# Retention and two feed-forward layers on one core: one written order, retention in pairs, smaller first-layer groups

## The chip, the core and the metric

The kernel runs on one core of a Trainium2 chip. A core has a matrix engine (TensorE, PE in the rows, with PEld for its weight loads), VectorE (DVE), ScalarE (ACT), GpSimd (POOL) and SyncE (SP), which issues the transfers (DMA). Matmuls write PSUM, eight banks of 2 KB per partition; all else works in SBUF. The metric is device time in microseconds (us); the span runs from the first to the last instruction of one profiled execution.

## The reference

```
for t in range(768):                                   # retention, 2 batches, 8 heads of 64
    state = gamma * state + k[t] (outer) v[t]
    y[t] = q[t] @ state / sqrt(64)
x = y as 1536 tokens x 512
h = x @ w_in   (512 x 2048);  g = softplus(h);  x = g @ w_out   (2048 x 512)
h = x @ w_in2  (512 x 2048);  g = h * sigmoid(h);  out = g @ w_out2
```

q, k, v are single precision, the weights double precision.

## The kernel before

**Retention.** The 768 positions are cut into 6 pieces of 128; with 2 batches that makes 12 chunks (chunk n is piece n // 2 of batch n % 2). For each chunk TensorE makes the scores of all heads (`att_scores`, L156: 8 matmuls, each over one half of the rows, which write two PSUM tiles), VectorE multiplies them by a decaying mask (L160), and TensorE multiplies them with v (the within-chunk part, `att_out`, L170: 8 matmuls, each into one half of the output partitions). To this it adds the across-chunk part, the scaled q times the state of all earlier pieces (L180: 4 full matmuls), in the same PSUM tile `py`. GpSimd scales q (L104) and k (L114). `att_state` multiplies scaled k with v in a PSUM tile (L130), and VectorE adds that to a block-diagonal state `sbd` in SBUF (L140, L142). ScalarE and VectorE split the result into a rounded part and the rest (xhi L195, xlo L196).

**Feed-forward.** Every operand is a pair (hi, lo), and a product is three matmuls. A step is one slice of 128 of the 2048 hidden channels for one block of 512 tokens (4 chunks): a first product of twelve matmuls into a PSUM tile `h` (`gemm1`, L277), an activation on ScalarE that writes it twice (`act1`, L293 and L294), the difference on VectorE (`act2`, L300), and, LAG = 2 steps later, a second product of twelve matmuls into four PSUM banks `acc` (`gemm2`, L319). Slices come in groups of 4; within a group the three blocks follow one another, and at the end of a block `acc` is added into `part` (`evacuate`, L334 to L338). There are 2 layers x 16 slices x 3 blocks = 96 steps.

**Weights.** Each of 64 weight tiles (32 slices, in and out) is loaded as raw 64-bit words (512 KB, three buffers) and converted: one ScalarE operation (L221), six on VectorE (`w_upper`, `w_lower`), one rounding copy on ScalarE (`w_split`, L256). `_convert_plan` says at which step.

**Order.** The opening and the first NFREE = 10 steps are ordered by a scheduler, which may mix independent parts on an engine; from step 10 on each engine follows the written order. All transfers go through SyncE's queue. The chunks' retention lies in the first steps: step i also carries chunk i + 5.

## Time and profile before

| | us |
|---|---|
| median of 3 runs | 602.47 (602.04 to 604.19) |
| the profiled execution | 602.17 |
| its span | 600.4 |
| TensorE busy | 585.1 (97%), 2946 matmul records |
| VectorE busy | 362.6 (60%) |
| ScalarE busy | 196.8 (33%) |
| GpSimd busy | 43.9 (7%) |
| transfers | 51.61 MB, 86 GB/s over the span |

A single-precision matmul shows as two records. A matmul's record is longer than the distance to the next, since matmuls are pipelined, so lengths of TensorE's work are read from starts. The granted clock says what share of full speed TensorE was given: 1.00 is 2.4 GHz, 0.50 is 1.2 GHz.

### The profile page before, as it was taken

The page shows a single profiled execution, that of the slowest core. Times are in us where ns is not written, and L with a number is a line of the kernel's source. Part 1 is how long each engine was busy: PE and PEld are TensorE (multiplying, and loading weights), DVE is VectorE, ACT ScalarE, POOL GpSimd, SP SyncE. Part 2 cuts the span into 40 slices and gives each one's busy share as a digit, 9 for nine tenths or more (in the row PEclk, how much of TensorE's full clock was granted, in tenths as well). Part 3 has the DMA queues.
Part 4 walks back from the last instruction along what each step waited for, and adds up shares of the span by engine and source line. Part 5 has one row for each costly group of instructions (what it writes and reads, how often), then busy time and mean ns, then how long its engine had stood idle before and what let it go on. Part 6 is the DMA issues. An engine that isn't in the chain of part 4 may idle for free.

```text
span 600.4 us, 7352 instructions
## 1 busy us (share of the span) xinstructions
PE 585.1 (97%) x2946; PEld 477.8 (80%) x2946; DVE 362.6 (60%) x622; ACT 196.8 (33%) x358; POOL 43.9 (7%) x36
## 2 busy tenths in 40 slices
PE   6999989999999999999999999999999999999997
PEld 3777767888888888888888888888888888888885
DVE  3899974145764757556766886365655775473332
ACT  1333322134322332333344543343333233332220
POOL 1343110000000000000032230000000000000000
PEclk9899989999999999999999999999999999999999
DMA  8883540012310311122221112131112122100111
GB/s 331 346 306 122 208 153 27 1 35 71 98 44 34 106 64 53 59 71 70 71 70 36 70 72 70 36 105 50 58 69 72 68 72 70 36 0 1 70 71 70
DMA packets 14145, 51.61 MB, mean 86 GB/s; under 512 B 1696, under 2 KB 1696, under 8 KB 12960
## 3 DMA queue, kind: packets, MB, share of 16 engines
q1 hardware_dynamic: 14112, 51.15, 23.8%
q8 instruction: 23, 0.38, 0.3%
q14 instruction: 10, 0.08, 0.0%
HBM read 48.00 MB, written 3.15 MB: 85 GB/s over the span
## 4 chain that ended last, share of the span: by engine, by line
PE 90%; DVE 6%; DMA 1%; issue 1%; ACT 0%; SPq 0%; DVEq 0%
PE acc L319 43%; PE h L277 42%; PE py L170 3%; PE py L180 2%; DMA mask<-in_mask 1%; DVE scm L160 1%; PE kv L130 1%; PE sc L156 1%; DVE sbd L142 1%; DVE m L238 1%; DVE glo L300 1%; DVE m L239 1%; DVE xlo L196 1%; DVE a L229 1%; DVE wlo L246 0%
## 5 line engine op out<-in xcount | busy, mean ns | idle before, releaser
L293 ACT ACTIVATE ghi<-h 128x512 fp32r<-128x512 f32 x96 | 57.4, 598 | 324.7 <-PE h L277 324.7
L226 DVE TENSOR_SCALAR z<-z 128x512 uint32<-128x512 uint32 x64 | 28.4, 444 | 115.7 <-ACT z L221 115.7
L300 DVE TENSOR_TENSOR glo<-t,ghi 128x512 fp32r<-128x512 f32 x96 | 66.6, 694 | 47.6 <-ACT t L294 47.6
L277 PE MATMUL h<-xhi,wlo 128*128 128x512 f32 (+1 forms) x196 | 76.0, 388 | 0.5 <-ACT xhi L195 0.5
L277 PE MATMUL h<-xlo,whi 128*128 128x512 f32 (+1 forms) x196 | 75.8, 387 | 0.0
L319 PE MATMUL acc<-ghi,wlo 128*128 128x512 f32 x192 | 75.8, 395 | 0.0
L277 PE MATMUL h<-xhi,whi 128*128 128x512 f32 (+1 forms) x196 | 75.7, 386 | 0.0
L319 PE MATMUL acc<-ghi,whi 128*128 128x512 f32 x192 | 74.9, 390 | 0.0
L319 PE MATMUL acc<-glo,whi 128*128 128x512 f32 x192 | 74.8, 390 | 0.0
L277 PE MATMUL h<-yhi,wlo 128*128 128x512 f32 x192 | 74.7, 389 | 0.0
L277 PE MATMUL h<-ylo,whi 128*128 128x512 f32 x192 | 74.7, 389 | 0.0
L277 PE MATMUL h<-yhi,whi 128*128 128x512 f32 x192 | 74.7, 389 | 0.0
L319 PE MATMUL acc<-whi,glo 128*128 128x512 f32 x192 | 74.7, 389 | 0.0
L319 PE MATMUL acc<-wlo,ghi 128*128 128x512 f32 x192 | 74.7, 389 | 0.0
L319 PE MATMUL acc<-whi,ghi 128*128 128x512 f32 x192 | 74.7, 389 | 0.0
L334 DVE TENSOR_TENSOR part<-acc,part 128x512 f32<-128x512 f32 x72 | 49.0, 691 | 34.3 <-PE acc L319 33.9
L294 ACT ACTIVATE t<-h 128x512 f32<-128x512 f32 x96 | 56.9, 593 | 0.0
L221 ACT ACTIVATE z<-raw 128x512 f32<-128x512 f32 x64 | 42.3, 663 | 24.1 <-DVE wlo L246 14.1
L256 ACT ACTIVATE whi<-a 128x512 fp32r<-128x512 f32 x64 | 40.4, 632 | 22.9 <-DVE a L229 22.9
L246 DVE SCALAR_TENSOR_TENSOR wlo<-m,z 128x512 fp32r<-128x512 int32 x64 | 44.8, 700 | 2.1
L239 DVE SCALAR_TENSOR_TENSOR m<-raw,m 128x512 uint32<-128x512 uint32 x64 | 44.3, 692 | 1.8
L229 DVE SCALAR_TENSOR_TENSOR a<-raw,z 128x512 uint32<-128x512 uint32 x64 | 44.3, 692 | 1.8
(42 smaller groups left out, 718.9 us busy)
## 6 DMA issues: line engine op xcount, KB each, us to landing
raw<-in_wts SPq DMA_DIRECT2D x64, 512.0 KB, 3.3
att<-in_att SPq DMA_DIRECT2D x9, 1024.0 KB, 6.5
out<-part SPq DMA_DIRECT2D x12, 256.0 KB, 2.1
att<-in_att SPq DMA_DIRECT2D x2, 768.0 KB, 10.6
qs<-in_qs SPq DMA_DIRECT2D x5, 256.0 KB, 6.2
att<-in_att SPq DMA_DIRECT2D x2, 512.0 KB, 6.0
mask<-in_mask SPq DMA_DIRECT2D x1, 512.0 KB, 8.6
att<-in_att SPq DMA_DIRECT2D x2, 256.0 KB, 9.3
```

What stands on the lines that cost most here:

```text
L221: nc.scalar.activation(out=z, in_=raw_t[u][:, :, 1].bitcast(F32), func=AF.Copy, scale=2.0**-112)
L226: nc.vector.tensor_scalar(out=z, in0=z, scalar1=3, scalar2=4, op0=ALU.logical_shift_left, op1=ALU.bitwise_or)
L229: nc.vector.scalar_tensor_tensor(out=a, in0=raw[:, :, 1], scalar=0x80000000, in1=z, op0=ALU.bitwise_and, op1=ALU.bitwise_or)
L239: nc.vector.scalar_tensor_tensor(out=m, in0=raw[:, :, 1], scalar=23, in1=m, op0=ALU.logical_shift_left, op1=ALU.bitwise_or)
L246: nc.vector.scalar_tensor_tensor(out=lo, in0=m.bitcast(I32), scalar=2.0**-43, in1=z, op0=ALU.mult, op1=ALU.mult)
L256: nc.scalar.activation(out=hi, in_=a, func=AF.Copy)
L277: nc.tensor.matmul(ph[:, t], lhsT=w[:, s], rhs=x[:, kc, t], start=kc == o == j == 0, stop=kc == NPAIR - 1 and j == 2, skip_group_check=i == 0,
L293: nc.scalar.activation(out=ghi, in_=ph, func=f)
L294: nc.scalar.activation(out=t, in_=ph, func=f)
L300: nc.vector.tensor_tensor(out=glo, in0=t, in1=ghi.bitcast(F32), op=ALU.subtract)
L319: nc.tensor.matmul(acc_t[m], lhsT=lhsT, rhs=rhs, start=(k == 0 and j == 0), stop=(k == GRP - 1 and j == 2))
L334: nc.vector.tensor_tensor(out=part[:, m, :], in0=acc_t[m], in1=part[:, m, :], op=ALU.add)
```

## The change

All engines now follow one written order from the first instruction on; no scheduler takes part. The chunks of the two batches of one piece go as a pair (`att_pair`): within 0 and 1, across 0 and 1 with their splits, then the scores of the next pair, the states, one copy of the state, the masks. The state is no longer added by VectorE: its matmuls accumulate over all pieces in one PSUM bank `state`, and ScalarE copies the bank to `past` in SBUF once per pair. The across part takes `past` by halves, 8 matmuls of 64 rows and 64 columns per chunk instead of 4 full ones. For chunks 0 and 1 a second ScalarE copy and a GpSimd subtraction make xlo (`spare`). The first layer's slices come in groups of 3, 3, 3, 3, 4. First products 0 to 4 lie between the pairs; the first second-product comes after the last pair. The weight plan is computed from the steps. Loads are issued in smaller pieces at first, in another order, and the last two chunks' second copy of k is not loaded.

```diff
-GRP = 4
-NGRP = NFC // GRP
+GROUPS = ((3, 3, 3, 3, 4), (4, 4, 4, 4))
+NSLOT = 6
 LAG = 2
-N = 2 * NGRP * NBLK * GRP
-NFREE = 10
 NRAW = 3
+NLEAD = 5
 WARM = 3
...
+def _steps():
+    steps = []
+    for l, sizes in enumerate(GROUPS):
+        f0 = 0
+        for g, size in enumerate(sizes):
+            steps += [
+                (l, g, b, f0 + k, k == 0, k == size - 1) for b in range(NBLK) for k in range(size)
+            ]
+            f0 += size
+    return steps
...
+    plan = [(0, 0, -2), (1, 0, -1), (2, 0, 0), (0, 1, 2), (1, 1, 3), (2, 1, 4)]
+    left = sorted(set(first) - {p[:2] for p in plan}, key=lambda u: (first[u], u))
+    at, credit = NLEAD, 1.0
+    while left:
+        ready = [u for u in left if last.get((u[0] - NSLOT, u[1]), -1) < at]
+        if ready and (credit >= 1 or first[ready[0]] <= at + 4):
+            u = ready[0]
+            assert at < first[u], (u, at, first[u])
+            left.remove(u)
+            plan.append((*u, at))
+            credit = max(0.0, credit - 1)
+        at += 1
+        credit = min(1.0, credit + 0.67)
...
-    gpool = ctx.enter_context(tc.tile_pool(name="gpool", bufs=LAG + 1))
+    gpool = ctx.enter_context(tc.tile_pool(name="gpool", bufs=LAG + 2))
...
+    state = ps.tile([P, B, NPAIR, D], F32, tag="st", bufs=1, name="state")
+    past = const.tile([P, B, NPAIR, D], F32, name="past")
...
-            if n in (0, 1, 2, 5, 6):
+            if n in (0, 1, 2, 5, 6, 7, 10, 11):
...
-                    pkv[j * D : (j + 1) * D, p, :],
+                    state[j * D : (j + 1) * D, b, p, :],
                     lhsT=kp[:, h, :],
                     rhs=a[:, 2, h * D : (h + 1) * D],
-                    start=True,
-                    stop=True,
+                    start=n == p == 0,
+                    stop=c == NCH - 2,
+                    skip_group_check=True,
                 )
-        for j in range(2):
-            r = slice(j * D, (j + 1) * D)
-            if c == 0:
-                nc.vector.tensor_copy(sbd[b][r, :, r], pkv[r])
-            else:
-                nc.vector.tensor_tensor(out=sbd[b][r, :, r], in0=pkv[r], in1=sbd[b][r, :, r], op=ALU.add)
+    def att_past():
+        nc.scalar.activation(out=past, in_=state, func=AF.Copy)
...
+        pj = [
+            psa.tile([P, NPAIR, P], F32, tag=f"acc{2 * (n % 2) + j}", name=f"sc{n}_{j}") for j in range(2)
+        ]
...
-            for p in range(NPAIR):
+    def att_across(n):
+        py, qp = py_t[n], qp_t.pop(n)
+        for p in range(NPAIR):
+            for j in range(2):
+                r = slice(j * D, (j + 1) * D)
                 nc.tensor.matmul(
-                    py[:, p, :],
-                    lhsT=sbd[b][:, p, :],
-                    rhs=qp_t[n][:, p, :],
+                    py[r, p, :],
+                    lhsT=past[r, n % B, p, :],
+                    rhs=qp[r, p, :],
                     start=False,
                     stop=(p == NPAIR - 1),
...
+        if spare:
+            full = epool.tile([P, NPAIR, P], F32, tag="t", name=f"y{n}")
+            nc.scalar.activation(out=full, in_=py, func=AF.Copy)
+            nc.gpsimd.tensor_tensor(out=lo, in0=full, in1=hi.bitcast(F32), op=ALU.subtract)
+        else:
+            nc.vector.tensor_tensor(out=lo, in0=py, in1=hi.bitcast(F32), op=ALU.subtract)
...
+    def att_pair(n):
+        more = n + B < NC
+        for b in range(B):
+            att_within(n + b)
+        for b in range(B):
+            att_across(n + b)
+            att_split(n + b)
+        if more:
+            for b in range(B):
+                att_scale_q(n + B + b)
+            for b in range(B):
+                att_scores(n + B + b)
+            for b in range(B):
+                att_state(n + b)
+            att_past()
+            for b in range(B):
+                att_mask(n + B + b)
+            if n + B < NC - B:
+                for b in range(B):
+                    att_scale_k(n + B + b)
...
+    def h_tag(i):
+        if i < NLEAD:
+            return "h"
+        if i < NLEAD + 3:
+            return ("st", "h", "py")[i - NLEAD]
+        return ("st", "py", "h", "py")[(i - NLEAD - 3) % 4]
...
+    def second(i):
+        gemm2(i, (0, 1))
+        evacuate(i, (0, 1))
+        gemm2(i, (2, 3))
+        evacuate(i, (2, 3))
+    def first(i):
+        gemm1(i, 0)
+        gemm1(i, 1)
+        act1(i)
...
+        att_load(0, 0, 2)
+        nc.sync.dma_start(out=mask, in_=mask_d)
+        att_load(1, 0, 2)
+        att_load(0, 2, 3)
+        att_load(1, 2, 3)
+        w_load(0)
+        att_load(2, 0, 2)
+        nc.sync.dma_start(out=cs, in_=cs_d)
+        att_load(0, 3, 4)
+        att_load(1, 3, 4)
...
+        att_scores(0)
+        att_mask(0)
+        att_scores(1)
+        att_mask(1)
+        att_within(0)
+        att_split(0, spare=True)
+        w_exponent(0)
+        att_within(1)
+        att_split(1, spare=True)
+        convert(0)
+        att_scores(2)
+        att_scale_k(0)
+        att_scale_k(1)
+        att_state(0)
+        att_state(1)
+        att_past()
...
+        w_digits(1)
+        att_split(2)
+        att_within(3)
+        att_across(3)
+        att_split(3)
+        gemm1(0, 0)
+        att_scale_k(2)
+        att_scale_k(3)
+        att_state(2)
+        att_state(3)
+        att_past()
...
+        gemm1(0, 1)
+        act1(0)
+        att_load(8)
+        qs_load(3)
+        att_scale_k(4)
+        att_scale_k(5)
+        w_exponent(2)
+        first(1)
+        convert(2)
+        act2(0)
+        act2(1)
+        att_pair(4)
+        att_load(9)
+        qs_load(4)
+        att_load(10, 0, 3)
+        for i, n in ((2, 6), (3, 8), (4, 10)):
+            u = units[i][0]
+            w_exponent(u)
+            first(i)
+            convert(u)
+            if i < NLEAD - 1:
+                act2(i)
+            att_pair(n)
+            if n == 6:
+                qs_load(5)
+                att_load(11, 0, 3)
+        second(0)
+        act2(4)
+        first(5)
+        for u in units[5]:
+            w_exponent(u)
+            convert(u)
+        second(1)
+        act2(5)
+        second(2)
+        first(6)
+        for u in units.get(6, ()):
+            w_exponent(u)
+            convert(u)
+        second(3)
+        act2(6)
+        second(4)
```

How TensorE's order changes around one chunk. Before, around chunk 7 (`py7` its output, `kv7` its state product, `h3` the first product of step 3):

```order
L170 MATMUL py7_637<-scm7_0_602,att7_371 64x128
L170 MATMUL py7_637<-scm7_1_604,att7_371 64x128
L180 MATMUL py7_637<-qp7_543,sbd1_88 128x128 x4
L130 MATMUL kv7_652<-att7_371,kp7_545 64x64 x8
L277 MATMUL h3_675<-xhi0_146,whi3_0_608 128x512
L277 MATMUL h3_675<-xhi0_146,wlo3_0_537 128x512
```

After, at the end of pair 4 (`sc7` are the scores of chunk 7, `state` the bank, `past` its copy, `h2` the first product of step 2), first the across part, then the end of the pair:

```order
L187 MATMUL py5_452<-scm5_1_381,att5_224 64x128
L201 MATMUL py4_443<-qp4_351,past_89 64x128 x8
L201 MATMUL py5_452<-qp5_353,past_89 64x128 x8
L169 MATMUL sc6_0_487<-att6_334 128x128
L169 MATMUL sc6_1_488<-att6_334 128x128
```

```order
L169 MATMUL sc7_1_498<-att7_336 128x128
L149 MATMUL state_88<-att4_114,kp4_403 64x64 x8
L149 MATMUL state_88<-att5_224,kp5_405 64x64 x8
L336 MATMUL h2_545<-xhi0_161,wlo2_0_433 128x512
L336 MATMUL h2_545<-xlo0_162,whi2_0_437 128x512
```

Before, across, state and product of one chunk follow one another, and products lie between the parts of a chunk. Now two chunks' across parts stand together, the next pair's scores come before the states, and a whole product follows. The across part has eight matmuls into 64 columns where it had four into 128.

GpSimd's first products (`kp` scaled k, `qp` scaled q, `y0` and `y1` the second copies of chunks 0 and 1). Before:

```order
L114 TENSOR_TENSOR kp0_135<-att0_89,cs_86 128x512
L114 TENSOR_TENSOR kp1_164<-att1_91,cs_86 128x512
L104 TENSOR_TENSOR qp2_188<-att2_98,qs2_99 128x512
L104 TENSOR_TENSOR qp3_245<-att3_102,qs2_99 128x512
L114 TENSOR_TENSOR kp2_289<-att2_98,cs_86 128x512
L114 TENSOR_TENSOR kp3_302<-att3_102,cs_86 128x512
```

After:

```order
L223 TENSOR_TENSOR xlo0_162<-y0_164,xhi0_161 128x4x128
L223 TENSOR_TENSOR xlo0_162<-y1_180,xhi0_161 128x4x128
L136 TENSOR_TENSOR kp0_203<-att0_92,cs_86 128x512
L136 TENSOR_TENSOR kp1_205<-att1_95,cs_86 128x512
L128 TENSOR_TENSOR qp2_238<-att2_101,qs1_106 128x512
L128 TENSOR_TENSOR qp3_240<-att3_108,qs1_106 128x512
```

The two subtractions for chunks 0 and 1 stand ahead of the scaled keys 0 and 1, which opened the queue before.

ScalarE after the last pair's product (`ghi4`, `t4` the activation of step 4, `whi2` a weight copy, `xhi2` the splits of chunks 10 and 11):

```order
L272 ACTIVATE z2_1_794<-raw2_1_435 128x512
L352 ACTIVATE ghi4_810<-h4_797 128x512
L353 ACTIVATE t4_811<-h4_797 128x512
L308 ACTIVATE whi2_1_824<-a2_1_795 128x512
L219 ACTIVATE xhi2_731<-py10_826 128x4x128
L219 ACTIVATE xhi2_731<-py11_835 128x4x128
L352 ACTIVATE ghi5_895<-h5_882 128x512
L353 ACTIVATE t5_896<-h5_882 128x512
```

Before, the splits of chunks 9 and 10 stood among the activations of steps 5 and 6 (`z`, `whi` weight tiles, `part` an evacuation):

```order
L256 ACTIVATE whi4_1_1035<-a4_1_973 128x512
L293 ACTIVATE ghi4_782<-h4_769 128x512
L294 ACTIVATE t4_783<-h4_769 128x512
L256 ACTIVATE whi5_1_1081<-a5_1_1038 128x512
L195 ACTIVATE xhi2_746<-py9_825 128x4x128
L293 ACTIVATE ghi5_870<-h5_857 128x512
L294 ACTIVATE t5_871<-h5_857 128x512
L336 ACTIVATE part0_0_899<-acc0_0_613 128x512
```

Now both splits of the last pair stand behind the activation of step 4. That one writes the buffer of step 0's activation, which the first second-product reads.

## Rows read from the trace of the kernel before

**Rows 1.** Windows: length, busy (count) of PE, PEld, DVE, ACT, POOL, clock, DMA, GB/s
```profile
0.00:106.48 106.48, 95.33 (x786) 72.55 (x787) 77.66 (x139) 31.60 (x53) 24.80 (x24) 0.95 0.57 211
106.48:596.12 489.64, 489.64 (x2161) 405.22 (x2159) 284.21 (x483) 165.17 (x305) 19.11 (x12) 1.00 0.17 59
596.12:600.40 4.28, 0.12 (x1) 0.00 (x0) 0.69 (x1) 0.00 (x0) 0.00 (x0) 0.95 0.32 123
```

**Rows 2.** The chain of waits after the prologue (start us, length us, what)
```profile
109.36 2.72 PE acc L319 x12
...
588.08 8.17 PE acc L319 x36
```

**Rows 3.** Timeline of TensorE around chunk 8 (start, length, line, tiles, idle time before)
```profile
65.10 1.16 PE L156 MATMUL sc<-att 64*128 64x128 f32 x16
66.19 0.50 PE L319 MATMUL acc<-ghi,wlo 128*128 128x512 f32 x1
66.53 0.40 PE L319 MATMUL acc<-glo,whi 128*128 128x512 f32 x1
...
67.77 1.43 PE L170 MATMUL py<-scm,att 128*64 128x128 f32 x16
69.14 1.16 PE L180 MATMUL py<-qp,sbd 128*128 128x128 f32 x8
70.23 0.69 PE L130 MATMUL kv<-att,kp 128*64 128x64 f32 x16
70.84 0.50 PE L319 MATMUL acc<-ghi,wlo 128*128 128x512 f32 x1
```

**Rows 4.** Timeline of TensorE, warm-up and first scores, and two of its waits
```profile
1.45 5.13 PE L383 MATMUL warm<-sbd 128*128 128x512 f32 x6 [1.45 <-DVE sbd L380]
6.51 2.35 PE L156 MATMUL sc<-att 64*128 64x128 f32 x32
11.53 0.43 PE L170 MATMUL py<-scm,att 128*64 128x128 f32 x2 [2.66 <-DVE scm L160]
...
80.52 0.43 PE L170 MATMUL py<-scm,att 128*64 128x128 f32 x2 [2.58 <-DVE scm L160]
```

**Rows 5.** Busy time in four windows with the granted clock, columns as in group 1
```profile
13.00:19.40 6.40, 5.20 (x60) 4.61 (x58) 5.19 (x11) 1.23 (x2) 3.56 (x4) 0.50 1.02 400
20.00:24.20 4.20, 4.20 (x46) 3.27 (x42) 4.20 (x8) 1.63 (x3) 1.04 (x1) 1.00 0.80 327
81.30:84.30 3.00, 3.00 (x20) 2.67 (x19) 2.24 (x5) 0.63 (x1) 0.00 (x0) 0.50 0.08 30
64.90:75.20 10.30, 10.30 (x84) 7.89 (x82) 10.22 (x18) 4.09 (x7) 2.47 (x2) 1.00 0.67 247
```

**Rows 6.** The chain of waits at the start and in the first half product
```profile
2.11 8.57 DMA mask<-in_mask
...
24.34 1.63 PE h L277 x12
```

**Rows 7.** Timeline of ScalarE: first weight slice, and one activation pair
```profile
12.06 0.69 ACT L221 ACTIVATE z<-raw 128x512 f32<-128x512 f32 x1 [10.04 <-DMA raw<-in_wts]
...
109.40 0.60 ACT L293 ACTIVATE ghi<-h 128x512 fp32r<-128x512 f32 x1 [3.52 <-PE h L277]
109.90 0.59 ACT L294 ACTIVATE t<-h 128x512 f32<-128x512 f32 x1
```

**Rows 8.** Timeline of VectorE: the first four mask products
```profile
10.78 2.48 DVE L160 TENSOR_TENSOR scm<-sc,mask 128x512 f32<-128x512 f32 x4 [8.84 <-DMA mask<-in_mask]
```

**Rows 9.** Groups of GpSimd (count, busy us, mean ns, idle before)
```profile
L358 POOL TENSOR_TENSOR ylo<-part,yhi 128x512 fp32r<-128x512 f32 x12 | 19.1, 1592 | 247.8 <-ACT yhi L357 247.8
L104 POOL TENSOR_TENSOR qp<-att,qs 128x512 f32<-128x512 f32 x10 | 13.8, 1386 | 47.5 <-DMA att<-in_att 31.9 <-issue 11.8 <-PE py L180 3.8
L114 POOL TENSOR_TENSOR kp<-att,cs 128x512 f32<-128x512 f32 x10 | 11.0, 1106 | 19.2 <-DMA cs<-in_cs 10.6 <-PE kv L130 7.7 <-DMA att<-in_att 1.0
```

**Rows 10.** The tile att: issue of a load to its landing
```profile
DMA to landing us min/median/max: 4.5/6.8/11.9
```

More of the change, by code (lines that the diff above doesn't have):

```diff
@@ L221, in w_exponent, with w_digits, w_values @@
         nc.scalar.activation(out=z, in_=raw_t[u][:, :, 1].bitcast(F32), func=AF.Copy, scale=2.0**-112)
-    def w_upper(u):
+    def w_digits(u):
+        w, s, _ = plan[u]
         raw = raw_t[u]
-        a, z = (t.bitcast(U32) for t in conv_t[u])
+        m = cpool.tile([P, DM], U32, tag="m", bufs=1, name=f"m{w}_{s}")
+        conv_t[u] += (m,)
+        nc.vector.tensor_scalar(out=m, in0=raw[:, :, 0], scalar1=9, scalar2=None, op0=ALU.logical_shift_right)
+        nc.vector.scalar_tensor_tensor(
+            out=m, in0=raw[:, :, 1], scalar=23, in1=m, op0=ALU.logical_shift_left, op1=ALU.bitwise_or
+        )
+    def w_values(u):
+        w, s, _ = plan[u]
+        raw = raw_t.pop(u)
+        a, z, m = conv_t[u]
+        a, z = a.bitcast(U32), z.bitcast(U32)
         nc.vector.tensor_scalar(
@@ L257, in w_split @@
         w_t[w, s] = (hi, w_t[w, s])
-    steps = [(l, g, b, g * GRP + k) for l in range(2) for g in range(NGRP) for b in range(NBLK) for k in range(GRP)]
     h_t, g_t, acc_t, part_t = {}, {}, {}, {}
+    def h_tag(i):
[4 more added lines that the diff above has]
+        return ("st", "py", "h", "py")[(i - NLEAD - 3) % 4]
     def gemm1(i, half):
-        l, g, b, fc = steps[i]
+        l, g, b, fc, _, _ = steps[i]
         if half == 0:
-            h_t[i] = ps.tile([P, BLK], F32, tag="att" if i >= NSTA and i % 4 > 1 else "h", name=f"h{i}")
+            tag = h_tag(i)
+            h_t[i] = ps.tile([P, BLK], F32, tag=tag, bufs=2 if tag == "py" else 1, name=f"h{i}")
         ph = h_t[i]
@@ L303, in gemm2 @@
     def gemm2(i, ms):
-        if i < 0:
-            return
-        l, g, b, fc = steps[i]
-        k = fc - g * GRP
+        l, g, b, fc, first, last = steps[i]
         ghi, glo = g_t[i]
@@ L319, in gemm2 @@
                 nc.tensor.matmul(
-                    acc_t[m], lhsT=lhsT, rhs=rhs, start=(k == 0 and j == 0), stop=(k == GRP - 1 and j == 2)
+                    acc_t[m], lhsT=lhsT, rhs=rhs, start=(first and j == 0), stop=(last and j == 2)
                 )
@@ L325, in evacuate @@
     def evacuate(i, ms):
-        if i < 0 or steps[i][3] % GRP != GRP - 1:
+        l, g, b, fc, _, last = steps[i]
+        if not last:
             return
-        l, g, b, fc = steps[i]
         if g == 0 and 0 in ms:
```

226 lines of the change are left out of this document (85 added, 141 removed).

## The prediction

> **What bounds the kernel now.** I read the three windows first [rows 1]. From 106.48 us to 596.12 us TensorE is busy for the whole 489.64 us at the full clock; before that it is busy for 95.33 of 106.48 us, and after it 4.28 us of evacuation and output remain. So there is a prologue, a solid middle and a tail. The chain of waits [rows 2] gives the unit of the middle: a product of twelve matmuls takes 2.72 us, and from the row at 109.36 to the row at 588.08 lie 478.72 us, which is 88 steps of two products (5.44 us). There are 96 steps, thus 192 products, 522.2 us in all. The middle holds 489.64 / 2.72 = 180 of them, so the prologue does 12, or 32.6 us, and spends 106.48 - 32.6 = 73.8 us on something else: the retention, the start, and waiting. The middle can't shrink, since no product is removed. The change is worth what it does to the 73.8 us, plus any stall that it puts into the middle.
>
> What TensorE needs of them: around chunk 8 [rows 3] the scores start at 65.10 and the next work at 66.19 (1.09 us), the within-chunk part takes 69.14 - 67.77 = 1.37 with a wait in it (1.17 estimated from its neighbours' lengths), the across part 70.23 - 69.14 = 1.09, the state 0.61. That is 3.96 us a chunk. Twelve chunks, the last two of them without state and the first two without across, need 44.1 us. With 6.5 us until the first scores [rows 4] this makes 50.6 of the 73.8. The other 23 us are waits and half-clock time. The timeline shows their kind [rows 4]: TensorE stands for 2.66 us and 2.58 us before within-chunk matmuls, and both times VectorE's masked scores release it. VectorE is busy 77.66 of the first 106.48 us [rows 1], as it converts twelve weight slices there, adds every chunk's state, and multiplies by the mask between them. After each of the two idle stretches the clock is granted at 0.50, which is 1.2 instead of 2.4 GHz, for 6.4 us and 3.0 us [rows 5]. I found no wait of length in the middle.
>
> **The change, part by part.**
>
> *Fewer things in front of the masks.* The state is summed in PSUM, so VectorE's additions go and ScalarE gets one copy per pair (0.60 us like its other copies of this size [rows 7]). Only six weight slices are converted before the last pair. The first second-product stands behind the last pair, so that the prologue holds 5 products (13.6 us), not 12. I now walk TensorE's written order.
>
> *Start.* Warm-up and first scores end at 6.5 + 2.35 = 8.9 us as before [rows 4]. The mask had 2.0 MB ahead of it and landed at 2.11 + 8.57 = 10.68 us [rows 6]; now 0.5 MB are ahead. At the 400 GB/s at which loads ran a little later [rows 5] 1.5 MB less is 3.7 us, so about 7.0 us; it is not last any more, because the scores of chunk 0 end at 7.7. The four mask products take 2.48 us [rows 8]: chunk 0's are there at 9.0, chunk 1's at 10.2. Within 0 and 1 follow until 11.4. The scores of chunk 2 need 3.0 MB, which before had landed at 12.06, when the first slice (its 3.0 MB too) was there [rows 7]: 12.1 to 13.2 us.
>
> *A new wait.* For chunks 0 and 1 ScalarE makes a second copy and GpSimd subtracts. Five ScalarE operations (two splits, two copies, the first exponent) at 0.5 to 0.6 us end at 13.1. GpSimd's second subtraction cannot start earlier, takes 1.4 us (between the products of 1.11 and 1.39 and the subtraction of 1.59 [rows 9]), and behind it in GpSimd's queue stand the two scaled keys at 1.1 us: 15.6 and 16.7 us. TensorE's state of chunk 0, and behind it everything, waits for them. It stands still from 13.2 to 15.6 and 0.4 us more, 2.8 us in all, and goes on at 17.3. That is as long as the two waits of before, so I expect half clock behind it. In the 6.4 us of half clock TensorE was busy for 5.20 [rows 5], work that half the time would have done: 2.6 us; I take 2.5 (bounds: 0, if the clock stays, and 3.2, half of the whole window).
>
> *To the first activation.* From 17.3: scores 3 (1.09), within and across of 2 and 3 (4.52), half a product (1.63 [rows 6]), states 2 and 3 (1.22), scores 4 and 5 (2.18), the other half (1.63): 12.3 us, so 29.6, with the half clock 32.1. Product 1 uses the same PSUM bank as product 0, so it waits for both activations of it, 1.1 us [rows 7]: 33.2.
>
> *Four products and four pairs.* Each of products 1 to 4 (2.72) has a pair behind it. A full pair is 2 x 3.96 + 0.2 for the changes between the two kinds of matmul = 8.1 us (after the scores the product's second matmul starts 0.34 us after its first, 66.19 to 66.53 [rows 3], where 2.72 / 12 = 0.227 is usual). The last pair has no scores and no state: 4.6. Sum 10.9 + 24.3 + 4.6 = 39.8, so 73.0 us. What hides the rest: per full pair VectorE has four masks (2.48 [rows 8]), two splits, six operations for a slice and one difference, all of this tile size; at the masks' 0.62 us the thirteen are 8.1 us against TensorE's 10.8, and the masks come while the next product runs; GpSimd has four products, 5.0 us. Were this cover gone, each of four pairs would wait for its masks, at most 2.5 us, ten in all.
>
> *The middle.* 187 products are left: 508.6 us. The activation of step 4 waits for the first second-product, as only four buffers hold activations; queued behind it on ScalarE are a weight copy and the splits of chunks 10 and 11, 2.9 us, which product 6 needs only 8.2 us later (three products lie between). Groups of three add twelve evacuations on VectorE, which is busy 284.21 of the 489.64 us [rows 1]; I count nothing for them. Behind the prologue, weight slices are due two to eight steps after their conversion begins. At two steps of 5.44 us the last copy is ready about 0.9 us ahead by my count, so a stall there would be under 1 us each, three places. Tail 4.28.
>
> Sum: 73.0 + 508.6 + 4.3 = 585.9 us of span. The profiled run took 602.17 us with a span of 600.40, so 1.8 lie around it: 587.7, called **588**, 14 us (2.4%) under both the profiled 602.17 and the median 602.47.
>
> **A rule against the change.** The across part was four full-array matmuls a chunk in 1.09 us, 0.27 each, where scores and within, eight half-array matmuls over as many columns, take 1.09 and 1.17, 0.14 each [rows 3]: two halves run side by side. Now it is eight matmuls with half the rows and half the columns, and no row shows that form. Bounds: 1.09 us a chunk if the two run side by side, 2.18 if not. I take 1.09, since the within part shows two halves writing one PSUM bank side by side. The Trainium skill (TensorEngine Tiling (Array Packing), Restrictions and Gotchas, Gotcha 1) says that row tiles write to different banks and can't use one bank at the same time; here both row halves write the same bank, at other partitions. Before, the scores obeyed it with two banks, so the trace doesn't test it; by that rule the price is the upper bound, and it makes the first rival.
>
> **The rivals.**
> *Quarter matmuls one after another:* ten chunks at 1.09 us more, 10.9 us, nothing to hide them as TensorE is the bound there: 598.7. For it: no row of that form. Against: halves overlap in both directions.
> *Late loads:* chunk 9's load goes out when state 4 frees its buffer, chunk 11's when state 6 does; each is needed 9.0 us later (a state, a product, 4.5 of within and across, a score). Loads landed after 4.5 to 11.9 us, 6.8 in the median [rows 10]. At 11.9 TensorE waits 2.9 us twice, and each wait brings 3.0 us at half clock, 1.5 lost [rows 5]: 8.8 more, 596.5. Against: the queue holds little else then.
> *Half clock through the pairs, the slower side:* a pair is 8 us of half-array work without a gap for products; in [rows 5] the clock stayed at 0.50 while TensorE did only such work. If it does so through the 39.8 us, they double: 627.5. It decides from 14.4 us of lost time on, that is when more than 14.4 us of this work runs at 1.2 GHz. Against: from 20.00 to 24.20 nothing but such work ran, at 1.00, and 64.90 to 75.20 stayed at 1.00 [rows 5].
>
> **How the numbers follow.** Forecast 0.70, quarter matmuls 0.15, late loads 0.10, half clock 0.05. The forecast's own range is 583 to 593: no half clock and quick subtractions take 3 to 5 off; loads 3 us later at the start, and small stalls in pairs and middle, add 5. To 8 in 10 I take in most of the rivals below no change: 582 to 598. What a measurement can tell from no change is 0.5%, 3.0 us, so 599.5. Under it lie the forecast, late loads, and most of the quarter case (598.7, with the forecast's spread around it): faster 0.90; within 0.06; slower 0.04.
>
> **What would show it.** Right: the last across matmul near 73 us, products 2.72 us apart from there on without a gap; the first state at 15 to 16 us, released by GpSimd's keys, and a 0.50 stretch after it; 1.1 us for eight across matmuls; VectorE well under nine tenths in slices up to 70 us. Wrong: across at 2.2 us; TensorE released by loads of chunk 9 or 11; waits for masks within pairs; gaps behind the groups of three; a granted clock of 0.50 beyond 25 us.

## The result, and the profile after

| | before | after |
|---|---|---|
| median | 603.15 us (602.04 to 604.19, 4 runs) | 584.55 us (583.81 to 584.77, 4 runs) |
| ratio | | 0.969, 95% interval 0.9668 to 0.9712 |
| profiled execution and its span | 602.17, 600.40 | 584.48, 582.30 |

The change makes the kernel 18.6 us (3.1%) faster. The forecast was 588.0 with a range of 582 to 598, so direction and range held, and the time lies 3.5 us under the forecast.

The three windows of the changed kernel, which answer to [rows 1] (length, busy time and count of PE, PEld, DVE, ACT, POOL, then clock, DMA share, GB/s):

```profile
0.00:69.50 69.50, 62.34 (x782) 51.55 (x782) 52.40 (x73) 21.70 (x37) 28.94 (x26) 0.95 0.75 270
69.50:578.30 508.80, 508.80 (x2246) 421.23 (x2244) 319.32 (x537) 177.20 (x328) 17.48 (x12) 1.00 0.19 63
578.30:582.30 4.00, 0.17 (x1) 0.00 (x0) 0.69 (x1) 0.00 (x0) 0.00 (x0) 1.00 0.34 131
```

Of the first 69.50 us five products take 13.6 (5 x 2.72), which leaves 55.9 for the retention, the start and waits, where it was 73.8. That is 17.9 us. The middle is 187 products: 187 x 2.72 = 508.6 against the measured 508.80, so not a single stall of note lies in it. The tail is 0.3 shorter. 17.9 + 0.3 - 0.2 = 18.0, which is the difference of the spans (18.1) but for 0.1. All of the gain lies in the prologue.

What kind of time went can be read from the same rows. TensorE's idle time in the prologue was 106.48 - 95.33 = 11.15 us [rows 1] and is 69.50 - 62.34 = 7.16: 4.0 us less. The other 13.9 us are busy time: without the products it was 95.33 - 32.6 = 62.7 us and is 62.34 - 13.6 = 48.7. Of that about 1 us is half clock (8.20 us of busy time at 0.50 in the two windows of [rows 5], 6.22 us now, and half of it is excess). So the larger part, about 13 us, is TensorE's own time for the retention and for the changes between it and the products.

A row of the chain of waits, beside [rows 2] (start, length, what):

```profile
72.56 2.72 PE h L336 x12
```

A product still takes 2.72 us; the middle is the same work, begun earlier.

TensorE from the scores of chunk 2 to the first states, beside [rows 4] (start, length, line, tiles, and the idle time before with what ended it):

```profile
12.90 1.16 PE L169 MATMUL sc<-att 64*128 64x128 f32 x16 [1.31 <-DMA att<-in_att]
16.07 1.07 PE L149 MATMUL state<-att,kp 128*64 128x64 f32 x16 [2.01 <-POOL kp L136]
17.52 1.12 PE L149 MATMUL state<-att,kp 128*64 128x64 f32 x16 [0.38 <-POOL kp L136]
```

The waits for VectorE's masked scores are gone (the trace of before has nine of them, 7.4 us in all). In their place stands a wait of 2.01 + 0.38 us for GpSimd's scaled keys, as forecast (2.8), and smaller ones for loads (1.31 here, 0.37 and 0.47 before it).

Two windows behind it, with the clock, and the three whole cycles of pair and product, columns as in the first view:

```profile
16.40:23.00 6.60, 6.22 (x66) 5.37 (x66) 6.44 (x9) 1.80 (x3) 5.12 (x4) 0.50 1.03 385
23.00:33.30 10.30, 9.20 (x136) 8.16 (x132) 8.06 (x11) 3.37 (x7) 6.44 (x6) 1.00 0.79 272
36.32:46.13 9.81, 9.81 (x141) 8.50 (x141) 7.66 (x11) 3.95 (x7) 3.84 (x4) 1.00 0.84 318
46.13:55.94 9.81, 9.81 (x142) 8.50 (x141) 9.67 (x15) 4.07 (x7) 6.58 (x5) 1.00 0.79 303
55.94:65.74 9.80, 9.80 (x141) 8.50 (x140) 8.65 (x17) 4.03 (x7) 2.50 (x2) 1.00 0.19 63
```

Half clock (0.50, which is 1.2 GHz) lasts 6.6 us behind the new wait; afterwards the clock stays at 1.00. In the three cycles TensorE is busy without a gap. VectorE is busy for 7.66, 9.67 and 8.65 us of about 9.81: in the second cycle, where GpSimd works longest, it is nearly the bound.

TensorE in one such cycle, from the pair of chunks 4 and 5 on, and at the end of the prologue, beside [rows 3]:

```profile
36.32 1.97 PE L187 MATMUL py<-scm,att 128*64 128x128 f32 x32
38.22 1.96 PE L201 MATMUL py<-qp,past 64*64 64x128 f32 x32
40.12 2.06 PE L169 MATMUL sc<-att 64*128 64x128 f32 x32
42.10 1.15 PE L149 MATMUL state<-att,kp 128*64 128x64 f32 x32
43.18 0.50 PE L336 MATMUL h<-xhi,wlo 128*128 128x512 f32 x1
...
67.64 1.96 PE L201 MATMUL py<-qp,past 64*64 64x128 f32 x32
69.54 0.50 PE L375 MATMUL acc<-ghi,wlo 128*128 128x512 f32 x1
```

From start to start: within 1.90, across 1.90, scores 1.98, state 1.08, together 6.86 us for two chunks. The forecast had 8.1. The first second-product starts at 69.54, forecast 73.0.

### The profile page after: what moved, and what is told of

Read it like the earlier page. It is cut to its first block, busy times and chain, and to the rows that moved or that the text cites. A ratio compares the mean times of both kernels' runs of the same rounds, so it can differ in the third digit from the quotient of the medians.

```text
span 582.3 us, 7525 instructions
## 1 busy us (share of the span) xinstructions
PE 571.3 (98%) x3026; PEld 472.8 (81%) x3026; DVE 372.4 (64%) x611; ACT 198.9 (34%) x365; POOL 46.4 (8%) x38
## 4 chain that ended last, share of the span: by engine, by line
PE 96%; DMA 1%; POOL 1%; ACT 0%; issue 0%; SPq 0%; DVE 0%; POOLq 0%
PE h L336 45%; PE acc L375 45%; PE py L187 2%; PE sc L169 2%; PE py L201 2%; DMA att<-in_att 1%; PE state L149 1%; POOL kp L136 0%; POOL xlo L223 0%; SPq L123 0%; DVE part L390 0%; ACT ghi L352 0%; ACT xhi L219 0%; ACT t L353 0%; ACT y L222 0%
## 5 line engine op out<-in xcount | busy, mean ns | idle before, releaser
L390 DVE TENSOR_TENSOR part<-acc,part 128x512 f32<-128x512 f32 x84 | 57.4, 692 | 50.0 <-PE acc L375 50.0
L289 DVE TENSOR_SCALAR z<-z 128x512 uint32<-128x512 uint32 x64 | 30.2, 472 | 71.1 <-ACT z L272 71.1
L353 ACT ACTIVATE t<-h 128x512 f32<-128x512 f32 x96 | 56.9, 593 | 0.0
L280 DVE SCALAR_TENSOR_TENSOR m<-raw,m 128x512 uint32<-128x512 uint32 x64 | 48.0, 749 | 2.2
L292 DVE SCALAR_TENSOR_TENSOR a<-raw,z 128x512 uint32<-128x512 uint32 x64 | 46.0, 719 | 2.2
L297 DVE SCALAR_TENSOR_TENSOR wlo<-m,z 128x512 fp32r<-128x512 int32 x64 | 46.0, 719 | 2.2
L336 PEld LDWEIGHTS h<-xhi,wlo 128*128 128x128 f32 x196 | 36.8, 188 | 9.1 <-ACT t L353 1.4
```

Source lines behind the costliest of these rows:

```text
L280: nc.vector.scalar_tensor_tensor(out=m, in0=raw[:, :, 1], scalar=23, in1=m, op0=ALU.logical_shift_left, op1=ALU.bitwise_or)
L289: nc.vector.tensor_scalar(out=z, in0=z, scalar1=3, scalar2=4, op0=ALU.logical_shift_left, op1=ALU.bitwise_or)
L292: nc.vector.scalar_tensor_tensor(out=a, in0=raw[:, :, 1], scalar=0x80000000, in1=z, op0=ALU.bitwise_and, op1=ALU.bitwise_or)
L297: nc.vector.scalar_tensor_tensor(out=lo, in0=m.bitcast(I32), scalar=2.0**-43, in1=z.bitcast(F32), op0=ALU.mult, op1=ALU.mult)
L336: nc.tensor.matmul(ph[:, t], lhsT=w[:, s], rhs=x[:, kc, t], start=kc == o == j == 0, stop=kc == NPAIR - 1 and j == 2, skip_group_check=i == 0,
L353: nc.scalar.activation(out=t, in_=ph, func=f)
```

## The experiments

Medians of four to six runs, in us, with the ratio to the kernel before on the same chip. "After" itself measured 584.55 and, run once more on the chip of e9 and e10, 585.21 (0.9669, 0.9627 to 0.971; 583.5 to 585 was expected). So a difference of less than about 1 us between medians of different chips decides nothing; there the trace has to speak.

| | median | ratio, 95% |
|---|---|---|
| e1 full across | 585.20 | 0.9674 (0.9637 to 0.9711) |
| e2 keys first | 582.63 | 0.9633 (0.9597 to 0.9668) |
| e3 fill | 583.86 | 0.9655 (0.9619 to 0.9692) |
| e4 half by half | 587.49 | 0.972 (0.9676 to 0.9763) |
| e5 before, as written | 624.36 | 1.0339 (1.0309 to 1.0369) |
| e6 groups of four | 597.23 | 0.9884 (0.9846 to 0.9923) |
| e7 VectorE additions | 591.73 | 0.9792 (0.9759 to 0.9824) |
| e8 four moves | 587.49 | 0.9723 (0.9694 to 0.9752) |
| e9 loads ahead | **579.44** | 0.9581 (0.9546 to 0.9615) |
| e10 keys loaded first | 585.66 | 0.968 (0.9643 to 0.9717) |

**e1: the across part as before, by full matmuls.** The state goes block-diagonally into `past` by two ScalarE copies.

```diff
-        nc.scalar.activation(out=past, in_=state, func=AF.Copy)
+        for j in range(2):
+            r = slice(j * D, (j + 1) * D)
+            nc.scalar.activation(out=past[r, :, :, r], in_=state[r], func=AF.Copy)
...
-            for j in range(2):
-                r = slice(j * D, (j + 1) * D)
-                nc.tensor.matmul(
-                    py[r, p, :],
-                    lhsT=past[r, n % B, p, :],
-                    rhs=qp[r, p, :],
+            nc.tensor.matmul(
+                py[:, p, :],
+                lhsT=past[:, n % B, p, :],
+                rhs=qp[:, p, :],
```

> The changed kernel with its across part as four full-array matmuls per chunk again: past is block-diagonal, written by two ScalarE copies per pair instead of one. Theory (the gain of the change comes from the waits that went, not from the form of the matmuls): eight quarter matmuls took 1.90 us per pair in the changed kernel; four full ones took 1.09 us per chunk before, of which some is overlap at the ends, so 1.9 to 2.2 us per pair, and the whole run 584.5 to 586.5 us. Rival (the quarter form itself brings a good part of the gain): over 2.6 us per pair, 588 us or more.

TensorE in a full pair (columns as above):

```profile
48.27 2.05 PE L200 MATMUL py<-qp,past 128*128 128x128 f32 x16
50.26 2.06 PE L170 MATMUL sc<-att 64*128 64x128 f32 x32
```

Eight full matmuls take 1.99 us from start to start, sixteen quarter matmuls 1.90. The form is worth 0.09 us a pair; the medians show no difference. So the quarter form neither costs nor earns anything that counts.

**e4: the same matmuls, one row half after the other.**

```diff
-        for p in range(NPAIR):
-            for j in range(2):
+        for j in range(2):
+            for p in range(NPAIR):
```

> The changed kernel with the across part's eight quarter matmuls in another order: the four of the one half first, then the four of the other, not in turns. Theory (the two halves run side by side when they take turns, although they write one PSUM bank): a matmul that follows one of its own half waits for it, so the eight take 1.7 to 2.2 us per chunk instead of 0.95, and the run is 7 to 12 us longer, 592 to 597 us. Rival (they run one after another anyway, each in 0.12 us): no change, 584.5 us.

The same view of this kernel:

```profile
49.09 2.56 PE L201 MATMUL py<-qp,past 64*64 64x128 f32 x32
51.59 2.06 PE L169 MATMUL sc<-att 64*128 64x128 f32 x32
```

2.50 us a pair instead of 1.90, that is 0.16 us per quarter matmul against 0.12 when the halves alternate. Five pairs make 3.0 us, and the median is 2.9 us above the first of "after" (2.3 above the second). The single records of the two traces show why (each matmul has two). In "after", from 38.22 us on, the records of the two halves start 6 to 7 ns apart, and such couples follow one another every 109 ns. Half by half, records of one half alone follow every 109 ns, until those of the next half begin between them; then they start 52 to 57 ns apart. So the two halves do run beside each other in one PSUM bank when they alternate, and half by half they still do for a part of the time. Both expectations missed: the cost is neither nothing nor that of two halves strictly in turn.

**e2: GpSimd's keys of chunks 0 and 1 ahead of the two subtractions.**

```diff
         att_scores(0)
         att_mask(0)
+        att_scale_k(0)
+        att_scale_k(1)
...
         att_scores(2)
-        att_scale_k(0)
-        att_scale_k(1)
```

> The changed kernel with one thing moved: GpSimd scales the keys of chunks 0 and 1 before it does the two subtractions, not behind them. Theory (the queue behind the subtractions makes TensorE stand before the first states, and the standing brings the half clock): the first state starts at about 14 us instead of 16.07, TensorE's 2.01 us wait for GpSimd goes or falls under 0.7, no stretch at 0.50 or a short one, and the run is 3 to 5 us shorter, 579.5 to 581.5 us. Rival (the keys' loads land late or the half clock comes from the earlier waits for loads): the wait is then put down to a load, the half clock stays, and the gain is under 1.5 us.

TensorE of this kernel, at the start and in product 3:

```profile
14.35 0.69 PE L149 MATMUL state<-att,kp 128*64 128x64 f32 x16 [0.64 <-POOL kp L136]
...
19.69 1.09 PE L201 MATMUL py<-qp,past 64*64 64x128 f32 x16 [1.32 <-POOL qp L128]
...
50.95 0.51 PE L336 MATMUL h<-xlo,whi 128*128 128x512 f32 x1 [0.52 <-DVE xlo L225]
```

The first state comes 1.7 us earlier and the mean clock of the run is 1.00: no half clock follows. But GpSimd's scaled queries are now late (1.32), and product 3 waits for VectorE. The median is 1.9 and 2.6 us under the two of "after", instead of the 3 to 5 expected; the first second-product starts at 67.27 instead of 69.54. The wait was real, and a part of it moved to the next thing in GpSimd's queue.

**e3: two matmuls on zeros in the gap**, which keep TensorE at work and change nothing else.

```diff
         att_scores(2)
+        fill = ps.tile([P, BLK], F32, tag="h", bufs=1, name="fill")
+        for _ in range(2):
+            nc.tensor.matmul(fill, lhsT=zero[:, :P], rhs=zero, start=True, stop=True)
```

> The changed kernel with two more matmuls of zeros (the warm-up's form, 0.85 us each at full clock) between the scores of chunk 2 and the first state; their result is read by nothing. Theory (TensorE's idle time before the first states brings the stretch of about 6 us at a granted 0.50, which costs about 2.6 us): with the gap filled from 14.0 to 15.7 us the clock stays at 1.00, and the run is 2 to 3 us shorter, about 582 us. Rival (the clock falls for the waits before, at 11.6 to 12.9 us, too, or for something else): the 0.50 stretch stays, and the time is the same or up to 1.5 us longer.

The window that was at half clock, in this kernel:

```profile
16.40:23.00 6.60, 5.48 (x96) 4.65 (x96) 6.04 (x9) 2.23 (x4) 5.53 (x5) 1.00 1.03 379
```

And its TensorE, at the states of chunks 0, 2 and 3 and in product 3:

```profile
17.02 0.69 PE L149 MATMUL state<-att,kp 128*64 128x64 f32 x16 [0.66 <-POOL kp L136]
...
25.66 1.15 PE L149 MATMUL state<-att,kp 128*64 128x64 f32 x32
...
52.80 0.50 PE L336 MATMUL h<-xlo,whi 128*128 128x512 f32 x1 [1.05 <-DVE xlo L225]
```

The same states of chunks 2 and 3 in "after":

```profile
27.45 1.15 PE L149 MATMUL state<-att,kp 128*64 128x64 f32 x32
```

The clock stays at 1.00. The first state starts 0.95 us later than in "after" and the states of chunks 2 and 3 start 1.79 earlier, so half clock had cost 2.7 us. Yet the first second-product starts only 0.4 us earlier (69.12), and the median is 0.7 us lower, about what two runs of one kernel differ by (0.66): product 3 waits 1.05 us for VectorE's xlo. That the earlier start brings this wait isn't shown. The second run of "after" has it too, with the pair before it at 46.35 (46.13 in the first run, which has none), and e1 has 0.88 us of it:

```profile
54.24 0.50 PE L336 MATMUL h<-xlo,whi 128*128 128x512 f32 x1 [0.52 <-DVE xlo L225]
```

In all these runs VectorE has little room in this cycle, and how long its operations take beside GpSimd's differs from run to run (L297 took 0.69 us there in the first run of "after" and 1.80 in the second).

**e7: the four additions per pair on VectorE again**, into a tile that nothing reads (20 of them, 0.42 us each).

```diff
         nc.scalar.activation(out=past, in_=state, func=AF.Copy)
+        z = zero.rearrange("p (b a d) -> p b a d", b=B, a=NPAIR)
+        for b in range(B):
+            for j in range(2):
+                r = slice(j * D, (j + 1) * D)
+                nc.vector.tensor_tensor(out=z[r, b], in0=state[r, b], in1=z[r, b], op=ALU.add)
```

> The changed kernel with four additions on VectorE behind every copy of the state, as large as those of the kernel before (64 partitions, 256 elements, from PSUM), 20 in all at 0.42 us; what they write is read by nothing. Theory (VectorE isn't the bound in the pairs any more, but near it, since it is slower while GpSimd works): about 1.7 us more per pair are hidden in part, 1 to 4 us longer, 585.5 to 588.5 us. Rivals: all hidden, 584.5 us; or all on the path, 8.4 us longer, 593 us.

Two windows of this kernel, columns as before:

```profile
17.40:27.40 10.00, 7.94 (x70) 6.76 (x72) 7.65 (x12) 2.03 (x4) 6.18 (x6) 0.50 1.02 393
48.50:60.00 11.50, 10.28 (x140) 8.26 (x139) 11.31 (x18) 3.83 (x7) 6.89 (x6) 1.00 0.71 269
```

And a wait of its TensorE:

```profile
22.59 2.36 PE L192 MATMUL py<-scm,att 128*64 128x128 f32 x16 [1.39 <-DVE scm L182]
```

6.5 to 7.2 us more (against the two medians of "after") for 8.4 us of additions, against the theory, which gave VectorE the room to hide most. It isn't one for one. 3.9 us are lost by product 1 (37.30 instead of 33.38), where the wait for the masks comes in the stretch at 0.50, which lasts 10.00 us instead of 6.6. In the pairs VectorE is busy 8.31 us of one cycle (37.30 to 48.50) and 11.31 of the 11.50 us shown, and product 3 waits 0.65 us for xlo. So taking the state out of VectorE is one of the main parts of the gain, worth up to 7 us in this order.

**e6: first-layer groups of four slices, as before.**

```diff
-GROUPS = ((3, 3, 3, 3, 4), (4, 4, 4, 4))
+GROUPS = ((4, 4, 4, 4), (4, 4, 4, 4))
...
-    plan = [(0, 0, -2), (1, 0, -1), (2, 0, 0), (0, 1, 2), (1, 1, 3), (2, 1, 4)]
+    plan = [(0, 0, -2), (1, 0, -1), (2, 0, 0), (3, 0, 2), (0, 1, 3), (1, 1, 4), (2, 1, 5), (3, 1, 6)]
...
-    at, credit = NLEAD, 1.0
+    at, credit = NLEAD + 2, 1.0
```

> The changed kernel with first-layer groups of 4, 4, 4, 4 instead of 3, 3, 3, 3, 4; product 3 then belongs to the first block, so its slice is converted in the second pair and the second weights of slices 2 and 3 follow at steps 5 and 6. Theory (three slices per group are what lets the second products start right behind the last pair: two more slices come too late): TensorE waits about 4 us twice, for the weights of the second products of steps 2 and 3, 590 to 596 us. Rival (the group size only adds evacuations, the weights come early enough): 583.5 to 585.5 us.

The second of two such waits of TensorE, with ScalarE and VectorE before it:

```profile
90.61 0.59 ACT L353 ACTIVATE t<-h 128x512 f32<-128x512 f32 x1
91.09 0.66 ACT L272 ACTIVATE z<-raw 128x512 f32<-128x512 f32 x1
91.78 0.43 DVE L289 TENSOR_SCALAR z<-z 128x512 uint32<-128x512 uint32 x1 [8.22 <-ACT z L272]
94.17 0.80 PE L375 MATMUL acc<-ghi,wlo 128*128 128x512 f32 x1 [4.09 <-DVE wlo L297]
```

A group of four needs a further weight slice converted in the first steps. Twice TensorE waits 4.09 us for one (the other time at 81.95), and both times the matmuls that follow run at half clock (records of 0.79 and 0.80 us instead of 0.50). Waits and half clock together are 12.0 to 12.7 us. The forecast had counted nothing for the groups: right for what they cost, but with groups of four in this order the early second products don't have their weights in time. VectorE isn't what is short: it had stood idle for 8.22 us, until ScalarE's operation on the slice (L272), which stands behind the activation of the step (L353) in the written order. Whether groups of four with the conversions in another place would be as fast wasn't tried, so the 12 us are the price of four in this place and not of the size alone.

**e5: the kernel before, with every engine in its written order.** Nothing else is changed: the whole body stands under `tc.manual_schedule()`.

> The kernel before with one edit: the opening and the first ten steps follow its written order too, no scheduler. Theory (the order alone brings little: as long as VectorE converts twelve slices, adds the states and makes the masks between, TensorE waits for masks): within 6 us of before, 598 to 609 us, with the masked scores still what releases TensorE. Rival (what the scheduler did was the fault, and any written order mends it): most of the 18.6 us, 585 to 592 us.

Its TensorE at the longest wait (the next is 5.92 us, of the same kind):

```profile
64.05 2.90 PE L156 MATMUL sc<-att 64*128 64x128 f32 x16 [7.47 <-DVE xlo L196]
```

20 us slower than before, more than the theory expected; that the order alone mends something is dead. The text of the old kernel has the pieces in an order that only the scheduler made good. A fixed order is no gain in itself. That the new sequence of pieces needs it is not shown: the new pieces were not run with the scheduler.

**e8: four moves at once.** The keys as in e2; the queries of chunks 2 and 3 ahead of the subtractions too; the second half of product 0 ahead of the scores of 4 and 5; and conversions behind the pair's masks instead of ahead of the pair, so that no mask stands behind a conversion.

```diff
             first(i)
+            att_pair(n)
             convert(u)
             if i < NLEAD - 1:
                 act2(i)
-            att_pair(n)
```

> The changed kernel with four moves in the written order: GpSimd scales keys 0 and 1 and queries 2 and 3 ahead of the two subtractions; the first product's second half goes before the scores of chunks 4 and 5, which then cover its activation; and in the loop over pairs the slice's conversion and the difference go behind the pair, not before it. Theory (each wait that the trace of the run with the keys first shows on TensorE can be covered: 1.3 us for the scaled query, 1.2 us for the activation, 0.8 us for the splits before product 3): 582.6 less 3.3, 578.5 to 580.5 us. Rival (a covered wait comes back elsewhere, on VectorE while GpSimd works, or as late loads): over 581.5 us.

TensorE at the scores of chunks 10 and 11:

```profile
59.40 2.08 PE L169 MATMUL sc<-att 64*128 64x128 f32 x16 [3.48 <-DMA att<-in_att]
```

The window of this kernel behind that wait:

```profile
59.00:66.00 7.00, 6.60 (x55) 5.76 (x56) 4.38 (x8) 1.67 (x3) 1.27 (x1) 0.52 0.04 7
```

The load of chunk 11 is late by 3.48 us, and half clock follows. This is the rival of the prediction called late loads, in another kernel. My reading was that the load stands on SyncE's queue behind a weight load, which waits for the raw buffer that a conversion frees, and the conversion had moved back. SyncE's queue in this trace bears it out:

```profile
51.69 0.33 SPq L264 DMA_DIRECT2D raw<-in_wts  x1
...
52.60 0.37 SPq L123 DMA_DIRECT2D att<-in_att  x1
```

From 39.17 to 51.69 nothing is issued. The weight load (51.69) goes when VectorE's last reading of the raw words ends (L292, 50.94 + 0.69), and chunk 11's load (52.60) right behind it; in e9 it goes at 47.83.

**e9: e8, with the last loads ahead of the conversion,** and the last pair's conversion in its old place.

```diff
             first(i)
+            if i == NLEAD - 1:
+                convert(u)
             att_pair(n)
-            convert(u)
-            if i < NLEAD - 1:
-                act2(i)
             if n == 6:
                 qs_load(5)
                 att_load(11, 0, 3)
+            if i < NLEAD - 1:
+                convert(u)
+                act2(i)
```

> The run with four moves, mended: the loads of query scale 5 and chunk 11 stand ahead of the slice's conversion, whose own load of a later slice waits in the same queue, and in the third round of the loop the conversion stands before the pair again. Theory (the run with four moves lost its gain to chunk 11's load alone, which waited in SyncE's queue behind a weight load that waited for VectorE: 3.5 us and half clock behind it): chunk 11's scores don't wait, TensorE reaches the first second-product at about 64.5 us instead of 69.54, and the run takes 578.5 to 580.5 us. Rival (another wait takes its place, VectorE's or a load's): over 581.5 us.

TensorE at the scores of chunks 10 and 11 and at the first second-product:

```profile
54.89 2.06 PE L169 MATMUL sc<-att 64*128 64x128 f32 x32
...
64.70 0.50 PE L375 MATMUL acc<-ghi,wlo 128*128 128x512 f32 x1
```

The fullest of its three cycles of pair and product:

```profile
51.10:60.90 9.80, 9.80 (x141) 8.50 (x140) 8.23 (x15) 4.00 (x8) 2.52 (x2) 1.00 0.18 61
```

VectorE is busy for 8.23 of 9.80 us there (7.40 and 5.90 in the two cycles before), where it was 9.67 of 9.81 in the fullest cycle of "after". No wait for the load, no half clock, and the first second-product starts at 64.70 instead of 69.54. That is the best version, 5.8 us under "after" on the same chip (579.44 against 585.21) and 25.8 under the kernel before. It confirms the reading of e8. What each of the four moves brings by itself was not tried, the keys (e2) apart.

**e10: e9, with the constants for the keys and the last parts of k loaded ahead of chunk 2 and the first weight slice,** so that the first states come sooner.

```diff
-        w_load(0)
-        att_load(2, 0, 2)
         nc.sync.dma_start(out=cs, in_=cs_d)
         att_load(0, 3, 4)
         att_load(1, 3, 4)
+        att_load(2, 0, 2)
+        w_load(0)
```

> That run with one more move: the small table of key scales and the keys of chunks 0 and 1 are loaded ahead of the first weight slice and of chunk 2's queries. Theory (in the run with the keys first GpSimd waited for the keys' load until 13.26 us): the keys are there about 1.5 us earlier, chunk 2 no later, and the first states start about 1.5 us earlier, 0.5 to 1.5 us less in all, 577.5 to 579.5 us. Rival (the first weight slice is then late for product 0 by as much): no change.

TensorE of this kernel:

```profile
13.81 1.15 PE L149 MATMUL state<-att,kp 128*64 128x64 f32 x32
...
21.89 2.52 PE L187 MATMUL py<-scm,att 128*64 128x128 f32 x16 [4.78 <-issue]
```

And its VectorE:

```profile
13.88 0.43 DVE L279 TENSOR_SCALAR m<-raw 128x512 uint32<-128x512 uint32 x1 [3.39 <-DMA raw<-in_wts]
...
16.48 1.63 DVE L292 SCALAR_TENSOR_TENSOR a<-raw,z 128x512 uint32<-128x512 uint32 x1
...
21.12 2.47 DVE L177 TENSOR_TENSOR scm<-sc,mask 128x512 f32<-128x512 f32 x4
```

The first states start 1.3 us sooner than in e9 (13.81 against 15.09), and the kernel is 6.2 us slower. The weight slice lands later, VectorE's conversion starts only at 13.88 (11.80 in e9), and the masks of chunks 2 and 3 stand behind it until 21.12 (16.68). Only 2.1 of these 4.4 us are the later load: the conversion itself takes 7.2 us instead of 4.9, as more of it now lies beside GpSimd's products. The 4.78 us that TensorE stands still are put down to "issue" and not to VectorE; that the masks are the cause is read from the times. TensorE is then at half clock. Theory and rival both missed it: neither had asked what else stands behind the load that is pushed back.

## Why the prediction was right, and where it was off

**The bound and the path: right.** The gain was to come from the prologue alone. It shrank by 17.9 us; middle and tail took 508.80 and 4.00 against 508.6 and 4.28.

**"The other 23 us are waits and half-clock time": too narrow.** TensorE's idle time in that prologue was 11.15 us, of which 1.45 lie before the warm-up, and half clock lengthened its work by about 4. That is 14 of the 23; the other 9 are work that took longer than 3.96 us a chunk and 2.72 a product. The forecast of the time didn't rest on the sentence, since it adds up the new order part by part. But the gain is for the larger part work that became shorter (13 us), and only for 4.0 us idle time that went.

**Start and new wait: right, in part by luck.** Scores of chunk 2 at 12.90 (forecast 12.1), first state at 16.07 (forecast 15.6), TensorE's stand 2.01 + 0.38 us (forecast 2.8), product 1 at 33.38 (forecast 33.2). The last agreement is in part luck: TensorE went on with the scores of chunk 3 at 18.57 where the forecast had 17.3, and needed 14.8 us from there to product 1 where it had 15.9. The chain of causes (GpSimd's subtractions stand ahead of the keys) is shown by e2. The half clock behind it cost 2.7 us by e3, forecast 2.5.

**"A full pair is 2 x 3.96 + 0.2 = 8.1 us, the last 4.6": mis-sized.** Measured 6.86 and 3.80. A cycle of pair and product took 9.81 us instead of 10.82; three of them make 3.0 us, the last pair 0.8, and the first product, 2.94 from start to start, takes 0.2 back. That is the 3.6 us by which 36.16 (from 33.38 to 69.54) lies under the forecast 39.8, and but for small terms the whole miss.

Part by part, a pair against two single chunks of [rows 3]: within 1.90 against 2.34, across 1.90 against 2.18, scores 1.98 against 2.18, state 1.08 against 1.22: 1.06 us less. The change between pair and product was sized well: a product of the cycle takes 2.95 instead of 2.72, forecast 0.2 more. What was wrong is that the parts of one chunk, each of 16 records between other kinds of matmul, were doubled. "After" holds both forms, since its chunks 2 and 3 still go one by one. TensorE at chunk 3:

```profile
23.78 1.09 PE L187 MATMUL py<-scm,att 128*64 128x128 f32 x16
24.81 1.09 PE L201 MATMUL py<-qp,past 64*64 64x128 f32 x16
25.83 0.39 PE L336 MATMUL h<-xhi,wlo 128*128 128x256 f32 x1
```

16 records take 1.03 and 1.02 us; 32 in a run take 1.90, not 2.05. So a change of kind costs about 0.15 us, and pairs save one in each of four kinds, 0.6 of the 1.06. Most of the rest is the within part, whose 1.17 I had estimated out of a row with a wait in it, where 1.03 would have been right.

**"VectorE 8.1 us against TensorE's 10.8": too favourable, without harm here.** Four masks take 2.48 us as before. But the conversion's operations are longer while GpSimd works. VectorE of "after":

```profile
41.47 2.48 DVE L177 TENSOR_TENSOR scm<-sc,mask 128x512 f32<-128x512 f32 x4
43.86 1.25 DVE L279 TENSOR_SCALAR m<-raw 128x512 uint32<-128x512 uint32 x1
45.14 1.42 DVE L280 SCALAR_TENSOR_TENSOR m<-raw,m 128x512 uint32<-128x512 uint32 x1
...
47.77 0.69 DVE L292 SCALAR_TENSOR_TENSOR a<-raw,z 128x512 uint32<-128x512 uint32 x1
```

GpSimd beside it:

```profile
44.78 2.68 POOL L136 TENSOR_TENSOR kp<-att,cs 128x512 f32<-128x512 f32 x2
```

While GpSimd's two products run, from 44.78 to 47.46, an operation of 0.69 us takes 1.42; as soon as they end, 0.69 again. VectorE came to 9.67 of 9.81 us in the cycle from 46.13 on. The other two cycles took 7.66 and 8.65. The prediction's own sign, VectorE well under nine tenths in slices up to 70 us, failed: of the page's slices of 14.6 us one there reads nine tenths. TensorE waited nowhere for VectorE in this trace of "after", but for 0.52 us in the second, and e7 shows how little room is left.

**The rivals.** *Quarter matmuls one after another* fell: 0.95 us a chunk (1.90 a pair). The Trainium skill's rule on it (TensorEngine Tiling (Array Packing), Restrictions and Gotchas, Gotcha 1) is not borne out in time for this form, in which the two row halves write different partitions of one bank: e1 and e4 show that alternating halves overlap. *Late loads* did not come in "after" (only waits of 0.37, 0.47 and 1.31 us at the start) but did in e8, at one of the two places that the rival named: 3.48 us where it had 2.9, and half clock over most of 7.00 us where it had 3.0. *Half clock through the pairs* fell: 1.00 from 23 us on.

**What the parts are worth** does not add up to 18.6, since each needs the others: the order alone -20 (e5), groups of three about 12 against groups of four in the same plan (e6), the state out of VectorE about 7 (e7), the quarter form nothing (e1). That the early second products need their weights ready in time is shown by e6. What made the work 13 us shorter is argued from rows: TensorE's records change from one line of the kernel to another 83 times in the prologue before and 30 times in "after", and 53 changes at 0.15 us are 8 us, an estimate. No run takes the pairs apart again. How the gain would split if the parts came one by one onto the kernel before was not tried.

## What to carry to other kernels

Take idle and busy time apart before the rest of a sum is called waits. Price a part in the company that it will have: a duration read beside a change of work holds that change, and grouping like work takes it out. When a wait goes, look for the next thing in the same queue, and when work is moved back, for every load and every buffer that its end releases (e8, e10). An engine that looks three quarters busy by its unhindered durations can be full in a stretch where another one works beside it.

## What the runs showed of the hardware

- VectorE's operations on two SBUF tiles took 1.4 to 1.8 us instead of 0.69 beside GpSimd's products (the longest one of L280 took 1.795, of the same operation in the kernel before 0.799), and those on one SBUF tile up to 1.52 instead of 0.42; masks, which read PSUM and one SBUF tile, stayed at 0.68 (0.62 from start to start). The Trainium skill (SBUF — State Buffer, SBUF: two separate sides) says that GpSimd and a VectorE operation with two SBUF inputs shut each other out of a shared port for a whole instruction. For the operations on two tiles the rows agree: they grew by 0.7 to 1.1 us, about the length of one product of GpSimd (1.0 to 1.7).
- A wait of 2.01 us with short stretches of work and idling around it was followed by 6.6 us at 0.50; filled with two matmuls on zeros, none followed. With waits of 4.09 (e6), 3.48 (e8) and 4.78 us (e10) the clock fell to 0.50 too; with single waits of 1.32 (e2), 1.05 (e3) and 0.88 us (e1) it didn't.
- Sixteen quarter matmuls took 1.90 us with the row halves in turn and 2.50 half by half; in turn, the records of the two halves start 6 to 7 ns apart.
